# Seven block products in place of eight for the output of the last two chunks

## The chip, the cores and the metric

The kernel runs on one core of a Trainium2 chip. The metric is the device time of one execution in microseconds (us). Names of engines in rows: PE is TensorE's matmuls and PEld its weight loads, DVE is VectorE, ACT is ScalarE, POOL is GpSimd, SP is SyncE; here SP and ACT issue the DMAs.

## What is computed

```python
def _attn_ref(q, k, v):                       # q, k, v: 8 batches x 8 heads x 576 x 64
    k_p = k.reshape(B, H, Sp, pool, D).mean(axis=3)      # pool = 8, Sp = 72
    v_p = v.reshape(B, H, Sp, pool, D).mean(axis=3)
    scores = scale * np.matmul(q, k_p.transpose(0, 1, 3, 2))
    scores = scores - np.max(scores, axis=-1, keepdims=True)
    attn = np.exp(scores)
    attn = attn / (np.sum(attn, axis=-1, keepdims=True) + 1e-09)
    return np.matmul(attn, v_p).astype(np.float32)

def _moe_ref(x, w_in, w_out):                 # x: 4608 x 512, w_in: 512 x 2048, w_out: 2048 x 512
    h = x @ w_in
    g = h * (1.0 / (1.0 + np.exp(-1.702 * h)))
    return (g @ w_out).astype(np.float32)
```

The attention's output, transposed to tokens x (heads, head dimension), is `x`.

## The kernel before, in words

The 4608 tokens are worked on in nine chunks of 512: chunk c from 0 to 7 is the first 512 tokens of batch c, chunk 8 is the 64 tokens left over of each batch. Attention of batch c runs between the dense products of earlier chunks and leaves `x` for chunk c. All dense products are in a 32-bit matmul format, each operand split into a high and a low part, so a product of two blocks is three matmuls: high by high, low by high, high by low.

Chunks 0 and 1 multiply plainly (`dense`). From chunk 2 on the first product, `x @ w_in`, is made pair by pair: a *pair* (function `pair`, p from 0 to 7) is 256 of the 2048 middle columns. Its four blocks (two blocks of 128 middle columns f by two halves th of the tokens) come from seven products of 42 matmuls of 256 columns in all (L2473, PSUM banks `ha` and `hb`), with sums of `x` and of `w_in` as operands. The sums of `w_in` were made once, stored in DRAM (`fold`) and are read again for each pair (`ws`, `shared`, L2405). Then `keep` copies a block out of PSUM (L2488, ACT or DVE), `plus` adds another bank's half to it (L2495, DVE), `gelu` makes the activation twice on ACT (L2512 in the rounded format, `gh`, and L2520 in full), and POOL or DVE subtracts to get the low part `gl` (L2527).

`outputs` is the second product, `g @ w_out`. For each pair there are eight products (two blocks f by four tiles of 128 tokens), each of three matmuls of 512 columns (L2675 to L2677), which add to four PSUM banks `o` for the whole chunk. The outputs of a pair stand between the products of the next pair. After the last pair `finish` copies each bank to SBUF and stores it; in chunk 8 the copies are made by DVE and ACT (L2234, L2246), and the last tile's two halves are stored on SP and on ACT at once (L2240).

The order of everything is that of a planner (`Plan.order`), which works from costs and due times; after it a table (`PLACES`) moves single steps by a number of places, and another (`SWAPPED`) gives single steps to the other engine of two (ACT or DVE, POOL or DVE). Each engine, and each DMA queue, then works strictly in that order.

## Time and profile before

| | |
|---|---|
| timed runs, median of 3 (lowest, highest) | 892.92 us (891.83, 893.32) |
| profiled execution, first to last instruction (its span) | 889.3 us |
| PE, DVE, ACT, POOL busy in the span | 878.7, 646.0, 544.2, 314.1 us |
| TensorE clock granted | full speed in all 40 slices |

The profiled execution has no time of its own but its span, which does not hold what lies around the program. The median of the timed runs is 3.6 us above that span, and this difference is what is added to a span to compare it with a time. A busy engine is one with an instruction under way; matmuls overlap each other, so the distance between their starts tells more than the busy time.

### The profile page before, as it was taken

To read this page: it belongs to the slowest core of one execution; us is meant where nothing else is said; L and a number is where in the kernel's file an instruction comes from. 1 tells how busy PE (TensorE), PEld (TensorE's weight loads), DVE (VectorE), ACT (ScalarE), POOL (GpSimd) and SP (SyncE) were. 2 spreads that over 40 slices of the span, in tenths; PEclk is the share of its full clock that TensorE was granted. 3 is DMA by queue.
4 is the path that set the end of the run, shared out by engine and by line. 5 is a ranking of instruction groups with operands and counts; after the bars stand their busy time and mean duration, and the time that the engine had idled before them with its cause. 6 is when DMAs were issued, how large, how long until landed. Compare 5 with 4: busy or idle time off the path is not lost.

```text
span 889.3 us, 15811 instructions
## 1 busy us (share of the span) xinstructions
PE 878.7 (99%) x5432; PEld 785.1 (88%) x5432; DVE 646.0 (73%) x1288; ACT 544.2 (61%) x1245; POOL 314.1 (35%) x309
## 2 busy tenths in 40 slices
PE   7999999999999999999999999999999999999997
PEld 6889888888899998899999998989998989998986
DVE  6998989888888886698878887787777843222332
ACT  5986755356676754667576766685568563344433
POOL 2888655564312233222421162236323460000000
PEclk9999999999999999999999999999999999999999
DMA  9954455657468757677776677678664675556541
GB/s 285 379 184 134 125 152 177 234 185 220 151 201 233 227 178 252 170 235 239 219 216 181 170 247 212 214 214 243 173 208 142 199 237 187 182 183 202 166 143 48
DMA packets 145263, 176.68 MB, mean 199 GB/s; under 512 B 85664, under 2 KB 96928, under 8 KB 145184
## 3 DMA queue, kind: packets, MB, share of 16 engines
q1 hardware_dynamic: 140336, 166.89, 61.2%
q10 hardware_dynamic: 4848, 8.78, 2.8%
q8 instruction: 43, 0.70, 0.3%
q14 instruction: 36, 0.29, 0.1%
HBM read 150.47 MB, written 25.17 MB: 198 GB/s over the span
## 4 chain that ended last, share of the span: by engine, by line
PE 94%; DVE 2%; ACT 1%; SPq 1%; DMA 1%; issue 1%; ACTq 0%
PE ha L2473 18%; PE hb L2473 13%; PE o L2677 12%; PE o L2676 12%; PE o L2675 11%; PE sps L1759 4%; PE h L2268 3%; PE h L2269 3%; PE h L2270 3%; PE o L2310 3%; PE o L2311 3%; PE o L2312 3%; PE pav L1998 1%; PE pav L2001 1%; PE pav L2000 1%; PE pav L1999 1%
## 5 line engine op out<-in xcount | busy, mean ns | idle before, releaser
L2677 PE MATMUL o<-w,glall 128*128 128x512 f32 x448 | 176.4, 394 | 0.0
L2675 PE MATMUL o<-w,ghall 128*128 128x512 f32 x448 | 176.4, 394 | 0.0
L2676 PE MATMUL o<-w,ghall 128*128 128x512 f32 x448 | 176.0, 393 | 0.0
L2527 POOL TENSOR_TENSOR glall<-shared,ghall 128x256 fp32r<-128x256 f32 x88 | 70.4, 805 | 215.1 <-ACT shared L2520 148.2
L2677 PEld LDWEIGHTS o<-w,glall 128*128 128x128 f32 x448 | 84.3, 188 | 18.5
L2473 PEld LDWEIGHTS ha<-xs,ws 128*128 128x128 f32 x672 | 92.7, 189 | 7.6 <-ACT shared L2488 1.0
L2473 PE MATMUL ha<-xs,ws 128*128 128x256 f32 x672 | 99.3, 284 | 0.0
L2512 ACT ACTIVATE ghall<-shared 128x256 fp32r<-128x256 f32 x150 | 61.5, 415 | 61.4 <-DVE shared L2495 30.4
L2473 PE MATMUL hb<-x,ws 128*128 128x256 f32 x672 | 95.5, 284 | 0.0
L2473 PEld LDWEIGHTS hb<-x,ws 128*128 128x128 f32 x672 | 89.1, 189 | 4.4 <-DVE shared L2495 0.5
L2675 PEld LDWEIGHTS o<-w,ghall 128*128 128x128 f32 x448 | 84.6, 189 | 9.1
L2676 PEld LDWEIGHTS o<-w,ghall 128*128 128x128 f32 x448 | 84.1, 188 | 9.1
L2495 DVE TENSOR_TENSOR shared<-shared,hb 128x256 f32<-128x256 f32 x112 | 46.5, 415 | 56.2 <-PE hb L2473 41.0
L2488 ACT COPY shared<-ha 128x256 f32<-128x256 f32 x94 | 34.8, 370 | 65.0 <-PE ha L2473 63.9
L2527 POOL TENSOR_TENSOR glall<-gall,ghall 128x256 fp32r<-128x256 f32 x45 | 33.3, 744 | 103.4 <-ACT gall L2520 67.9
L2268 PE MATMUL h<-x,w 128*128 128x256 f32 (+1 forms) x192 | 63.1, 328 | 0.8 <-ACT g L2285 0.5
L2520 ACT ACTIVATE shared<-shared 128x256 f32<-128x256 f32 x150 | 61.0, 415 | 3.7 <-ACT osb L2228 0.5
L2269 PE MATMUL h<-x,w 128*128 128x256 f32 (+1 forms) x192 | 61.2, 319 | 0.0
L2270 PE MATMUL h<-x,w 128*128 128x256 f32 (+1 forms) x192 | 61.2, 319 | 0.0
L2298 POOL TENSOR_TENSOR gl<-g,gh 128x512 fp32r<-128x512 f32 x30 | 40.2, 1340 | 48.0 <-ACT gh L2290 33.2
L2527 DVE TENSOR_TENSOR glall<-shared,ghall 128x256 fp32r<-128x256 f32 x62 | 29.2, 472 | 36.0 <-ACT shared L2520 30.5
L2473 PEld LDWEIGHTS ha<-x,shared 128*128 128x128 f32 x336 | 46.7, 189 | 4.9 <-ACT shared L2488 0.8
(194 smaller groups left out, 2057.2 us busy)
## 6 DMA issues: line engine op xcount, KB each, us to landing
ws<-wd SPq DMA_DIRECT2D x168, 512.0 KB
shared<-wd SPq DMA_DIRECT2D x56, 256.0 KB
out_dram<-osb ACTq DMA_DIRECT2D x32, 256.0 KB
wd<-stage SPq DMA_DIRECT2D x16, 512.0 KB
raw<-in_moe_w_in_dram SPq DMA_DIRECT2D x15, 512.0 KB
raw<-in_moe_w_out_dram SPq DMA_DIRECT2D x15, 512.0 KB
kv_False<-in_k_dram SPq DMA_DIRECT2D x28, 256.0 KB
kv_True<-in_v_dram SPq DMA_DIRECT2D x28, 256.0 KB
```

The costliest lines, as they stand in the source:

```text
L2268: nc.tensor.matmul(o, lhsT=w[:, 0, j], rhs=xs[:, 0], start=j == 0, stop=False)
L2269: nc.tensor.matmul(o, lhsT=w[:, 1, j], rhs=xs[:, 0], start=False, stop=False)
L2270: nc.tensor.matmul(o, lhsT=w[:, 0, j], rhs=xs[:, 1], start=False, stop=j == NJ - 1)
L2298: engine.tensor_tensor(out=gl(), in0=g(), in1=gh().bitcast(F32), op=ALU.subtract)
L2473: nc.tensor.matmul(o, lhsT=wv()[:, r, jj], rhs=xo(k, jj), start=start and n == 0, stop=n == len(terms) - 1,  skip_group_check=not start,)
L2495: lambda: nc.vector.tensor_tensor(out=part(i), in0=part(i), in1=hb()[:, half * 256 : half * 256 + 256], op=ALU.add),
L2512: lambda: nc.scalar.activation(out=gh(), in_=src(), func=AF.Gelu_apprx_sigmoid),
L2520: lambda: nc.scalar.activation(out=part(i), in_=src(), func=AF.Gelu_apprx_sigmoid),
L2527: engine.tensor_tensor(out=gl(), in0=part(i), in1=gh().bitcast(F32), op=ALU.subtract)
L2675: nc.tensor.matmul(o(), lhsT=gh()[:, tok], rhs=w()[:, 0], start=start, stop=False)
L2676: nc.tensor.matmul(o(), lhsT=gh()[:, tok], rhs=w()[:, 1], start=False, stop=False)
L2677: nc.tensor.matmul(o(), lhsT=gl()[:, tok], rhs=w()[:, 0], start=False, stop=stop)
```

## The change

In chunks 7 and 8 (`SEVEN`), except for the last pair of chunk 8, the second product is made as the first one already is: for a pair, the two blocks of `g` by two halves of the tokens and the two blocks of `w_out` by two halves of its columns give seven products (P1 to P7) in place of eight. Each of the seven (`sevens`) is six matmuls of 256 columns.

- Four sums of blocks of `g` are needed per pair (`combined`: s1 to s4): a subtraction or addition on DVE, a rounding copy on ACT or DVE, and a subtraction on POOL or DVE for the low part. The rounded activation of one of the four blocks is no longer needed.
- Four sums of blocks of `w_out` are needed per pair (t1 to t4). They are made once (`make_sums`), during chunks 2 to 5, in 32 sets of three additions or subtractions (POOL or DVE), one copy (ACT or DVE) and one store to DRAM (SP). In chunks 7 and 8 they are read back, two reads of 512 KB per pair (`fetch_sums`), into space that attention no longer uses.
- P1, P5, P6 and P7 add up in the four banks `o` over the chunk, and P3 in a bank of its own. P2 and P4 share one bank (`Z`) by turns, and are added to a sum in SBUF by DVE after each pair (`add_up`).
- After the last pair the output's four quadrants are put together from these sums on DVE (`end`), and stored for chunk 7 as two stores of 512 KB. In chunk 8 the last pair is made by `outputs` as before, in the banks `o` again, and DVE adds each of them to the quadrants (`finish_sum`).
- More places for `g` and its parts are added from attention's space (`g_slot`, `c_slot`), and `PLACES` and `SWAPPED` have new numbers, from the end of chunk 1 on.

```diff
--- before.py
+++ after.py
-    "ACT ah0_0#0": 15.003, "ACT ah0_0#1": 14.024, "ACT ah0_0#2": -11.989, "ACT ah0_0#3": -38.996,
...
+    "ACT ah0_0#0": 15.36, "ACT ah0_0#1": 16.88, "ACT ah0_0#2": -8.6154, "ACT ah0_0#3": -35.0, "ACT ah0_1#0": 11.0,
...
+    SEVEN = (7, 8)
+    MADE = 2
...
     def finish(c, t, acc):
...
+        if c == B:
+            return finish_sum(t, acc)
...
+        def store():
+            nc.vector.tensor_tensor(out=osb(), in0=acc(), in1=osb(), op=ALU.add)
+            queues = (nc.sync, nc.scalar) if t == CHUNK - P else (nc.scalar,) * 2 if t == P else (nc.sync,) * 2
...
     def pair(c, p, due, then):
...
-        keep(0, ha)
+        begun = keep(0, ha)
+        if seven:
+            plan.due = due - 20
+            sums[c, p] = fetch_sums(c, p, begun)
...
+        def combined(name, op, i, a, b):
+            plan.due = due - EAGER
+            t = dve(
+                256,
+                lambda: nc.vector.tensor_tensor(out=part(i), in0=part(a), in1=part(b), op=op),
+                [at(a), at(b)],
+                [at(i)],
+                port=True,
+            )
+            hold(t, *[places[k][1] for k in {i, a, b}])
+            gh, w1 = g_slot(f"{nm}_{name}", "gh", True)
+            gl, w2 = g_slot(f"{nm}_{name}", "gl", True)
+            hold(copy(256, lambda copy: copy(out=gh(), in_=part(i)), [at(i)], [gh], sbuf=True), w1, places[i][1])
+
+            def rest(engine):
+                engine.tensor_tensor(out=gl(), in0=part(i), in1=gh().bitcast(F32), op=ALU.subtract)
+
+            t = pool(256, lambda: rest(nc.gpsimd), [at(i), gh], [gl], other=lambda: rest(nc.vector))
+            hold(t, w2, places[i][1])
+            return gh, gl
+
+        ops = {"11": got[0, 0], "12": got[1, 0], "22": got[1, 1]}
+        for name, op, i, a, b in (
+            ("s1", ALU.add, 2, 1, 2),
+            ("s3", ALU.subtract, 1, 0, 1),
+            ("s2", ALU.subtract, 0, 2, 0),
+            ("s4", ALU.subtract, 3, 3, 0),
+        ):
+            ops[name] = combined(name, op, i, a, b)
+        return ops
...
+    def make_sums(p):
+
+        def parts(i, cols):
+            h = homes[1, 2 * p + i]
+            return h, lambda: h()[:, :, 256 * cols : 256 * cols + 256].bitcast(F32)
+
+        left = {}
+        for name, a, b, op in (
+            ("t3", parts(1, 1), parts(0, 1), ALU.subtract),
+            ("t2", "t3", parts(0, 0), ALU.add),
+            ("t4", "t2", parts(1, 0), ALU.subtract),
+            ("t1", parts(0, 1), parts(0, 0), ALU.subtract),
+        ):
+            d = buf(moe, [P, 2, 256], F32, "osb", f"made{p}_{len(left)}")
...
+            step(512, d, av, bv, op, [a, b], [d])
+            step(256, lambda d=d: d()[:, 1], lambda d=d: d()[:, 0], lambda d=d: d()[:, 1], ALU.add, [], [d])
+            other = ("DVE", 0.2, lambda high=high: high(nc.vector.tensor_copy), True)
+            made.add("ACT", 0.32, lambda high=high: high(nc.scalar.copy), [], [d], other=other)
+            step(
+                256,
+                lambda d=d: d()[:, 1].bitcast(F32R),
+                lambda d=d: d()[:, 1],
+                lambda d=d: d()[:, 0],
+                ALU.subtract,
+                [],
+                [d],
+            )
+            i, k = next((i, ts.index(name)) for i, ts in enumerate(TS) if name in ts)
+            made.add(
+                "DMA",
+                0.8,
+                lambda d=d, i=i, k=k: nc.sync.dma_start(out=t_dram[p][i][:, k], in_=d()),
+                [d],
+                [(t_refs[p][i], k)],
...
+            b = Buf(ring, view, f"ts{c}_{p}_{i}")
+            t = dma(
+                P * 4096,
+                lambda b=b, i=i: nc.sync.dma_start(out=b().bitcast(F32), in_=t_dram[p][i]),
+                [],
+                [b],
+                lag=LAGS["ws"],
+            )
+            hold(t, whole)
+            plan.behind(t, begun)
+            t_fetches.append((t, p, i))
...
+        todo = [
+            ("P1", "11", of(w0, 0)),
+            ("P2", "12", of(w1, 0)),
+            ("P6", "s2", ts["t2"]),
+            ("P7", "s3", ts["t3"]),
+            ("P5", "s1", ts["t1"]),
+            ("P4", "22", ts["t4"]),
+            ("P3", "s4", of(w1, 1)),
+        ]
...
+        def add_up(name, z):
+            c_of = sums_of[c, name]
+            plan.due = due - 5.0
+            if first:
+                copy(512, lambda copy: copy(out=c_of(), in_=z()), [z], [c_of])
+            else:
+                dve(512, lambda: nc.vector.tensor_tensor(out=c_of(), in0=c_of(), in1=z(), op=ALU.add), [z], [c_of])
...
+                def products(gh=gh, gl=gl, wv=wv, bank=bank, fresh=fresh):
+                    w = wv()
+                    for i in range(2):
+                        o, tok = bank()[:, 256 * i : 256 * i + 256], slice(P * i, P * i + P)
+                        for k, (g, r) in enumerate(((gh, 0), (gh, 1), (gl, 0))):
+                            begin = fresh and i == 0 and k == 0
+                            nc.tensor.matmul(
+                                o,
+                                lhsT=g()[:, tok],
+                                rhs=w[:, r],
+                                start=begin,
+                                stop=k == 2,
+                                skip_group_check=not (fresh and i == 0),
+                            )
+
+                t = pe(6 * 120, products, [gh, gl, wb], [bank], mode="f32r")
+                hold(t, *[x for x in (whole, wh) if x is not None])
+                if name in ("P2", "P4"):
+                    add_up(name, bank)
+                if last:
+                    plan.due = due + at + n * step - 3.0
+                    end(name)
...
+            if is_seven(c, p):
+                then = sevens(c, p, acc, got, sums[c, p], due + ROUND / NPAIR)
+            else:
+                then = outputs(c, p, acc, got, due + ROUND / NPAIR)
...
+    for n, t in enumerate(made.tasks):
+        n, k = divmod(n, 5)
+        begin, end = (at[f"PE ha{MADE + n // 8}_{i}#2"] for i in (0, 7))
+        t.rank = begin + (end - begin) * (n % 8 + 0.2 * k + 0.3 * (k == 4)) / 8
```

In all, PE loses 360 matmuls of 512 columns and gets 630 of 256 columns (15 pairs of 24 and of 42).

PE in chunk 7 around the start of pair 4's products, before. `ha7_4` and `hb7_4` are pair 4's products from `x`; `o7_...` are outputs of pair 3 (`w1_6` and `w1_7` are its two blocks of `w_out`).

```order
L2473 MATMUL hb7_4_9018<-x7_8148,ws7_4_0_8858 128x256 x6
L2473 MATMUL ha7_4_9028<-x7_8107,ws7_4_0_8858 128x256 x6
L2473 MATMUL hb7_4_9018<-x7_8478,ws7_4_1_8890 128x256 x6
L2675 MATMUL o7_0_8709<-w1_7_841,ghall0_2956 128x512
L2676 MATMUL o7_0_8709<-w1_7_841,ghall0_2956 128x512
L2677 MATMUL o7_0_8709<-w1_7_841,glall0_2969 128x512
L2675 MATMUL o7_256_8759<-w1_7_841,ghall1_2996 128x512
L2676 MATMUL o7_256_8759<-w1_7_841,ghall1_2996 128x512
L2677 MATMUL o7_256_8759<-w1_7_841,glall1_3006 128x512
L2473 MATMUL ha7_4_9028<-xs7_15_8540,ws7_4_2_8920 128x256 x6
L2675 MATMUL o7_128_8773<-w1_6_824,ghall0_2956 128x512
L2676 MATMUL o7_128_8773<-w1_6_824,ghall0_2956 128x512
L2677 MATMUL o7_128_8773<-w1_6_824,glall0_2969 128x512
```

The same place in the changed kernel. `bankP3` is P3 of pair 2, `o7_0_P1` is P1 of pair 3, `bankZ` with `sums_main` is P4 of pair 2.

```order
L2619 MATMUL ha7_4_9302<-x7_8270,ws7_4_0_9180 128x256 x6
L3088 MATMUL bankP3_9124<-w1_5_781,ghmore_ah0_8966 128x256 x2
L3088 MATMUL bankP3_9124<-w1_5_781,glmore_al0_8968 128x256
L3088 MATMUL bankP3_9124<-w1_5_781,ghmore_ah0_8966 128x256 x2
L3088 MATMUL bankP3_9124<-w1_5_781,glmore_al0_8968 128x256
L3088 MATMUL o7_0_P1_8973<-w1_6_840,ghmore_ah1_8980 128x256 x2
L3088 MATMUL o7_0_P1_8973<-w1_6_840,glmore_al1_9004 128x256
L3088 MATMUL o7_0_P1_8973<-w1_6_840,ghmore_ah1_8980 128x256 x2
L3088 MATMUL o7_0_P1_8973<-w1_6_840,glmore_al1_9004 128x256
L2619 MATMUL hb7_4_9331<-x7_8403,ws7_4_0_9180 128x256 x6
L3088 MATMUL bankZ_8949<-sums_main_8866,ghall0_2967 128x256 x2
L3088 MATMUL bankZ_8949<-sums_main_8866,glall0_2983 128x256
```

Where three matmuls of 512 columns stood there are now six of 256, and the outputs stand further behind the products from `x`: P3 and P4 of pair 2 come while pair 4 is under way.

DVE at the end of the program, before: the last additions and low parts of pair 7 of chunk 8, and two of the four copies of the result.

```order
L2527 TENSOR_TENSOR glall0_2969<-gall_3057,ghall0_2956 128x256
L2495 TENSOR_TENSOR shared12_2917<-shared12_2917,hb8_7_10074 128x256
L2527 TENSOR_TENSOR glall1_3006<-shared12_2917,ghall1_2996 128x256
L2495 TENSOR_TENSOR gall_3057<-gall_3057,hb8_7_10074 128x256
L2527 TENSOR_TENSOR glall0_2969<-shared12_2917,ghall0_2956 128x256
L2527 TENSOR_TENSOR glall1_3006<-gall_3057,ghall1_2996 128x256
L2234 COPY osb8_0_10164<-o8_0_9466 128x512
L2234 COPY osb8_256_10178<-o8_256_9538 128x512
L2735 UNCONDITIONAL_BRANCH
```

And in the changed kernel:

```order
L3018 TENSOR_TENSOR u8_10753<-u8_10753,o8_0_P5_10056 128x512
L3018 TENSOR_TENSOR both8_0_10788<-u8_10753,bankP3_9124 128x2x256
L2642 TENSOR_TENSOR gall_3067<-gall_3067,hb8_7_10755 128x256
L2680 TENSOR_TENSOR glall1_3035<-csmore_tl_8868,ghall1_3007 128x256
L3018 TENSOR_TENSOR both8_1_10864<-v8_10857,o8_0_P5_10056 128x2x256
L2680 TENSOR_TENSOR glall1_3035<-csmore_tl_8868,ghall1_3007 128x256
L2680 TENSOR_TENSOR glmore_al0_8968<-gall_3067,ghmore_ah0_8966 128x256
L2382 TENSOR_TENSOR both8_0_10788<-o8_0_10870,both8_0_10788 128x512
L3006 TENSOR_TENSOR sum8_P4_10066<-sum8_P4_10066,bankZ_8949 128x512
L3018 TENSOR_TENSOR both8_1_10864<-v8_10857,sum8_P4_10066 128x2x256
L2382 TENSOR_TENSOR both8_1_10864<-o8_256_10881,both8_1_10864 128x512
L2382 TENSOR_TENSOR both8_1_10864<-o8_384_10885,both8_1_10864 128x512
L2382 TENSOR_TENSOR both8_0_10788<-o8_128_10902,both8_0_10788 128x512
```

The copies have become additions of `o8_...` to `both8_0` and `both8_1` (the quadrants), the sums for P3, P4 and P5 stand among the last low parts, and the last of all is the tile at token 128, whose two stores stand one behind the other on ACT.

## Rows read from the trace of the kernel before

**Rows 1.** The page's busy times, and slices of the span in tenths.

```profile
PE 878.7 (99%) x5432; PEld 785.1 (88%) x5432; DVE 646.0 (73%) x1288; ACT 544.2 (61%) x1245; POOL 314.1 (35%) x309
...
PE   7999999999999999999999999999999999999997
...
DVE  6998989888888886698878887787777843222332
```

**Rows 2.** The page's chain that ended last, by engine.

```profile
PE 94%; DVE 2%; ACT 1%; SPq 1%; DMA 1%; issue 1%; ACTq 0%
```

**Rows 3.** Waits of PE from 238 to 884 us: total, times, longest.

```profile
PE ha L2473 <- DVE gall L2488: 0.2, 1, 0.2
```

**Rows 4.** Chain through chunk 8, 794.47 to 884.2 us: by line, and pieces.

```profile
by line: PE ha L2473 25.6%; PE hb L2473 19.4%; PE o L2677 18.5%; PE o L2675 18.4%; PE o L2676 18.2%
...
862.79 1.44 PE hb L2473 x12
...
867.02 0.70 PE ha L2473 x6
...
868.42 0.80 PE ha L2473 x6
...
870.63 0.81 PE hb L2473 x6
```

**Rows 5.** Windows of the same stretch, of L2473 and of L2675 alone.

```profile
794.47:884.20 89.73, 46.16 (x336) 1.00 0.45 144
...
794.47:884.20 89.73, 28.21 (x72) 1.00 0.45 144
```

**Rows 6.** Windows by chunk: us, busy PE, PEld, DVE, ACT, POOL, clock, DMA share, GB/s.

```profile
238.00:333.00 95.00, 95.00 (x608) 86.00 (x607) 80.10 (x169) 61.65 (x149) 24.81 (x26) 1.00 0.66 202
333.00:428.00 95.00, 94.82 (x606) 85.99 (x605) 74.60 (x157) 64.10 (x160) 28.67 (x34) 1.00 0.72 223
523.00:614.50 91.50, 91.50 (x593) 82.95 (x591) 72.95 (x145) 64.67 (x160) 33.77 (x37) 1.00 0.72 215
794.47:884.20 89.73, 89.73 (x552) 80.25 (x551) 28.43 (x69) 38.32 (x95) 0.00 (x0) 1.00 0.45 144
```

**Rows 7.** Groups of instructions: count, busy us, mean ns, idle before and its end.

```profile
L2495 DVE TENSOR_TENSOR shared<-shared,hb 128x256 f32<-128x256 f32 x112 | 46.5, 415 | 56.2 <-PE hb L2473 41.0 <-ACT shared L2488 14.4
L2527 DVE TENSOR_TENSOR glall<-gall,ghall 128x256 fp32r<-128x256 f32 x29 | 15.2, 522 | 24.9 <-ACT gall L2520 24.9
L2076 DVE TENSOR_TENSOR xt<-xt,xt 128x512 f32<-128x512 f32 x7 | 7.0, 996 | 0.3 <-POOL xt L2076 0.2
L2082 DVE CAST x<-xt 128x512 fp32r<-128x512 f32 x8 | 4.3, 543 | 1.5 <-POOL xt L2076 1.4
...
L2527 POOL TENSOR_TENSOR glall<-shared,ghall 128x256 fp32r<-128x256 f32 x88 | 70.4, 805 | 215.1 <-ACT shared L2520 148.2 <-PE ha L2473 44.4 <-issue 7.1
L2076 POOL TENSOR_TENSOR xt<-xt,xt 128x512 f32<-128x512 f32 x14 | 19.7, 1405 | 14.4 <-DVE xt L2052 10.5 <-ACT xt L2052 3.6
```

**Rows 8.** PE in order of time around 377 us.

```profile
377.19 0.97 PE L2473 MATMUL ha<-x,shared 128*128 128x256 f32 x6 [0.18 <-DVE gall L2488]
```

**Rows 9.** The DMA queue's own waits on SP in chunk 8.

```profile
SPq L2405 <- PE ha L2473: 39.2, 12, 5.2
SPq L2405 <- PE hb L2473: 18.6, 12, 4.5
```

**Rows 10.** The end in order of time, 881.96 us on: copies of the result and their stores.

```profile
881.96 0.69 DVE L2234 COPY osb<-o 128x512 f32<-128x512 f32 x1 [0.92 <-PE o L2677]
...
883.26 1.19 ACTq L2236 DMA_DIRECT2D out_dram<-osb  x2
...
884.27 0.40 PE L2677 MATMUL o<-w,glall 128*128 128x512 f32 x1
884.71 0.58 ACT L2246 COPY osb<-o 128x512 f32<-128x512 f32 x1 [1.48 <-PE o L2677]
885.32 0.47 ACTq L2240 DMA_DIRECT2D out_dram<-osb  x1
885.47 0.55 SPq L2240 DMA_DIRECT2D out_dram<-osb  x1
```

More of the change, by code (lines that the diff above doesn't have):

```diff
@@ L2524, in gelu @@
             )
+            hold(t, places[i][1])
+            if late:
+                return None
             def rest(engine):
                 engine.tensor_tensor(out=gl(), in0=part(i), in1=gh().bitcast(F32), op=ALU.subtract)
-            if c == B:
+            if c == B and not seven:
                 t = dve(256, lambda: rest(nc.vector), [at(i), gh], [gl], port=True)
```

228 lines of the change are left out of this document (182 added, 46 removed), and 1840 rows, old and new, of tables (PLACES, SWAPPED).

## The prediction, made before the result was known

> **What bounds the kernel now.** I read the busy times first: PE is busy 99% of the span and its slices are full from the second to the last but one [rows 1], and PE makes up 94% of the chain that ended last [rows 2]. Since matmuls overlap, "busy" could hide waits, so I asked next for the waits of PE from the first pair of chunk 2 to the last product: one, of 0.2 us [rows 3]. Shorter waits show in the chain, where six matmuls from `x` take 0.72 us each time they follow each other (1.44 for twelve) but 0.80 or 0.81 in two places of chunk 8 [rows 4]. So between 238 and 884 us the time is the number of matmuls times their distance, with next to nothing lost. The reader is to see two consequences: matmuls that go away are time that goes away, if nothing new makes PE wait; and a new order of the steps has almost no waiting left to remove.
>
> **The products.** I price a matmul by the chain through chunk 8, which is 89.73 us long and nothing but PE [rows 4]. The lines of `ha` and `hb` have 25.6 + 19.4 = 45.0% of it, 40.4 us, and the windows count 336 such matmuls [rows 5]: 0.1202 us for 256 columns. The three lines of the output have 55.1%, 49.4 us, and 72 matmuls each, 216 in all [rows 5]: 0.2289 us for 512 columns. A matmul of half the columns costs a little more than half. The shapes that the change adds are those of `ha` and `hb` (128 by 128 stationary, 256 columns, a fresh weight load each), so their row is the price.
>
> Per pair, out go 24 x 0.2289 = 5.49 us, in come 42 x 0.1202 = 5.05 us: 0.445 us less. With the shortest piece of six in that chain, 0.70 [rows 4], it would be 0.59. Fifteen pairs are 6.7 us by the mean and 8.9 by the shortest piece. **I take -6.9 us**: a mean over 336 is what 630 will be near to, and it holds a few small waits that I cost apart. One product of eight is an eighth of the output's share in two chunks, but half of that comes back because short matmuls are dearer per column.
>
> **The sums of g, in chunks 7 and 8.** Per pair there are four additions, four roundings and four low parts more, one rounding by ACT and one low part less, and two additions of 512 columns for bank Z. I counted the changed order over its 15.5 pairs: DVE has per pair some 1.3 copies, 3.1 `plus`, 3.5 low parts, 3.9 sums, 1.9 roundings and 1.8 additions from bank Z. At 0.42 us for those with 256 columns (0.415 where one input is in PSUM, 0.522 for the low part, which has both in SBUF [rows 7]), half of 0.543 for a rounding [rows 7] and 0.69 for 512 columns out of PSUM [rows 10], that is 0.5 + 1.3 + 1.8 + 1.6 to 2.0 + 0.5 + 1.2 = 6.9 to 7.3 us of a pair's 10.1 us. Before, DVE was busy 28.4 us in the eight pairs of chunk 8, 3.6 us a pair, and POOL not at all [rows 6]; POOL gets 3.6 low parts a pair at 0.805 [rows 7], 2.9 us. So the engines have the time; the question is when each result is there. The longest chain is: last product of a pair, `plus`, activation, s1, s2, rounding, low part, P6: 0.42 + 0.42 + 0.42 + 0.42 + 0.3 + 0.8 and five hand-overs, about 4 us by these rows. In the changed order some twenty products (14 us) stand between a pair's last product and its P6 in the middle of a chunk, and eight to ten (6 to 7 us) at a chunk's start and end; the eight places for `gh` and `gl` in place of four allow it. Tighter is bank Z: it is used twice a pair, and four times in the two chunks only two products, 1.4 us, lie between two uses, against 0.17 (what a matmul's row reaches beyond the next start, 0.40 less 0.23 [rows 10]) and 0.69 us of DVE, which must begin within half a us. What is queued behind an addition that waits for Z on DVE are the next low parts, for which PE waits; that is where a miss would show. The bound from below is no wait; from above I take one wait per pair like the 0.80 or 0.81 in place of 0.72 [rows 4], 15 x 0.09 = 1.3 us, or at two per pair 2.7. **+0.5 us**, nearer the lower end, since chunk 8 of before shows two such pieces in eight pairs.
>
> **The sums of w_out, in chunks 2 to 5.** 32 sets of three steps on POOL or DVE: by the order 15 of 512 columns and 26 of 256 go to DVE, 17 and 38 to POOL, and the table moves 24 combining steps of `x` (512 columns) from POOL to DVE. At 0.996 and 0.522 us on DVE and at 1.405 and 0.805 on POOL [rows 7], DVE gets 15 + 14 + 24 = 53 us more, POOL 24 + 31 - 34 = 21 us more, over chunks 2 to 6; a dozen copies that go from DVE to ACT give some 5 us back. DVE is busy 73 to 80 us of a chunk's 91 to 95 now [rows 6]; with 10 more it is at 83 to 90. The cover is that none of these sums is needed before chunk 7; what is not covered are the steps queued behind them on DVE, on which PE waits. From below nothing; from above, each of the 32 sets delays PE once like the one wait that the rows show (0.97 us for six matmuls in place of 0.72 [rows 8]): 8 us. That DVE's 15 to 20 idle us a chunk are not used up puts it near the lower end: **+0.4 us**. The 32 stores (256 KB) add 8 MB to some 80 MB in those chunks (380 us at 202 to 223 GB/s [rows 6]), and the 30 reads of 512 KB some 105 GB/s to 144 GB/s at a share of 0.45 [rows 5]: 0.78 if it scales. SP's reads wait for PE to free a buffer, 24 times in chunk 8 [rows 9], and are issued most of a pair ahead of their use, so 1 or 2 us more of transfer is hidden. I cost them at nothing; without that lead each late read would cost PE 1 to 2 us.
>
> **The end.** The last tile's copy was 0.58 us on ACT, and its two stores were issued side by side, 0.47 and 0.55 us [rows 10]. Now DVE adds it, 0.69 us by its copy of the same size, and both stores of the tile that is last (token 128) are issued by ACT one behind the other; two such took 1.19 us [rows 10], 0.5 more than the 0.7 from the first issue to the second one's end. **+0.6 us.** The four banks are handed from P1, P6, P7, P5 to the last pair's tiles while three more products run (2.1 us), behind one to three additions of 0.69: no wait by this count, at most 1 us.
>
> Sum: -6.9 + 0.5 + 0.4 + 0.6 = -5.4 us. The profiled execution's 889.3 becomes 883.9; with the 3.6 us around it, 887.5 us. That is 0.6% under the median of 892.92. A measurement of this kernel can tell some 0.2% (1.8 us) from no change.
>
> **Rivals.**
> *VectorE falls behind in chunks 7 and 8* (the gain is lost). For it: 7 us of 10, most of it in chains, on an engine with a strict order. A step of 256 columns takes DVE 0.415 with one input in PSUM and 0.522 with both in SBUF [rows 7], and one of 512 columns 0.69 out of PSUM [rows 10] and 0.996 with both in SBUF, so something beside it costs DVE a quarter or more there. The Trainium skill ("SBUF — State Buffer", "Who interferes with whom") says why: a VectorE instruction with two SBUF inputs and a GpSimd one that reads SBUF take turns, and the second waits for the whole of the first; this trace's means agree. Against it: POOL works 2.9 us of 10. If a third of its 7.4 such steps of a pair met a POOL step and lost half of 0.8 us, DVE would be at 8.3 us a pair, still under 10.1. It decides from 10.1 on: at 10.55 us a pair all of the gain is gone (15 x 0.445) and the time is 893 to 894.
> *The sums of w_out hold up PE in chunks 2 to 5* (the other sign). From 32 sets at 0.17 us on, the gain of 5.4 us is eaten; at the full 0.25 of the one wait shown it is +8 in place of +0.4 and the time 895. For it: DVE is the busiest engine after PE just there, and a rounding on ACT waits in line for a step on POOL. Against it: PE waited 0.2 us in all those chunks although DVE was at 80 of 95 us.
> *Half of either*, 2 to 4 us lost: 889.5 to 891.
> *Cheaper still*: the short price for every matmul and no new waits, 892.9 - 8.9 + 0.6 = 884.6.
> That the change does not do what it says is ruled out by the order: 360 matmuls out, 630 in.
>
> **How the numbers follow.** Forecast, 885.5 to 889.5: 0.62. Cheaper still, under 885.5: 0.12. Half lost, 889.5 to 891.1: 0.10. No gain, within 0.2% either way: 0.09. Slower, by one of the first two rivals in full: 0.07. So faster by over 0.2% 0.84, within 0.2% 0.09, slower 0.07. The range reaches to the ends of the cheap and the half lost case, 884.3 to 891.2, and leaves out about 0.18.
>
> **What would show it.** Right: 630 matmuls at 0.12 us and a pair in chunks 7 and 8 of 10.1 to 10.2 us in place of 10.55; PE's waits between 238 us and the end still under 1 us in sum; DVE busy about 7 us a pair at the end; the store of the last tile 0.6 us later behind the last matmul. Wrong: a pair of 10.4 us or more with PE waiting for `gl` or for bank Z; PE waits on DVE or ACT in chunks 2 to 5 that add to several us; matmuls from DRAM's sums that wait for a read.

## The result, and the profile after

The change made the kernel slower: 899.91 us (898.50 to 901.72, four runs) against 892.38 us (890.86 to 893.32, four runs), a ratio of 1.0091 with a 95% interval of 1.0071 to 1.0110. The forecast was 887.5 us, 884.3 to 891.2. The profiled execution has a span of 899.1 us and a time of 900.92.

Busy times and the waits of PE come first, as in [rows 1, 3]. From the page of the changed kernel:

```profile
PE 880.2 (98%) x5702; PEld 796.6 (89%) x5702; DVE 729.7 (81%) x1518; ACT 553.2 (62%) x1287; POOL 341.8 (38%) x357
...
DVE  6998989888979988777888888898778657667666
...
PE 86%; DMA 6%; SPq 3%; ACT 2%; DVE 1%; issue 1%; POOL 0%; ACTq 0%; DVEq 0%; POOLq 0%
```

PE is busy all but as before, yet it makes up 86% of the chain where it was 94% [rows 2], and DMA has come in with 6%. Waits of PE from 238 to 894 us (total, times, longest):

```profile
PE ha L2619 <- DMA shared<-wd: 3.7, 1, 3.7
PE hb L2619 <- DVE shared L2642: 2.4, 2, 2.2
PE kps L1687 <- DVE xs L2184: 1.1, 1, 1.1
PE ha L2619 <- ACT shared L2634: 0.6, 2, 0.4
PE ha L2619 <- DMA ws<-wd: 0.5, 1, 0.5
PE o L2865 <- POOL glall L2680: 0.2, 1, 0.2
```

One wait of 0.2 us [rows 3] has become eight with 8.5 us, and none of them lies in chunks 7 and 8. The windows say where (us, busy PE, PEld, DVE, ACT, POOL, granted clock, DMA share, GB/s): chunk 2, chunk 3, chunk 4, and a stretch of chunk 8.

```profile
241.00:338.00 97.00, 95.11 (x597) 85.70 (x596) 84.41 (x183) 64.76 (x158) 25.61 (x29) 0.98 0.74 232
338.00:444.00 106.00, 99.89 (x610) 88.76 (x609) 82.42 (x178) 66.51 (x162) 35.54 (x41) 0.97 0.70 208
444.00:538.00 94.00, 93.42 (x599) 83.95 (x598) 79.64 (x173) 67.15 (x165) 30.77 (x34) 1.00 0.76 233
...
810.00:890.00 80.00, 80.00 (x668) 79.70 (x667) 56.98 (x136) 34.98 (x93) 23.32 (x32) 1.00 0.71 253
```

Chunk 3 takes 106 us for as many matmuls as 95 us held before [rows 6]. The granted clock, full throughout before, is below it in two chunks. The longest stall shows how one leads to the other; in order of time, around 396 us:

```profile
391.31 0.59 SPq L2540 DMA_DIRECT2D shared<-wd  x1
...
395.47 0.40 PE L2865 MATMUL o<-w,glall 128*128 128x512 f32 x1
...
399.58 1.42 PE L2619 MATMUL ha<-x,shared 128*128 128x256 f32 x6 [3.72 <-DMA shared<-wd]
```

The six matmuls at 399.58 wait for a read of 256 KB that was issued at 391.3 us, and then take 1.42 us; six such matmuls at full clock read 0.88 in this view (at 404.28 us), which has the last one's whole length in it. The windows of 4 us there:

```profile
392.00:396.00 4.00, 3.77 (x21) 2.64 (x19) 3.86 (x10) 2.17 (x3) 1.61 (x2) 1.00 0.94 239
396.00:400.00 4.00, 0.41 (x3) 0.45 (x4) 0.76 (x3) 3.02 (x6) 1.53 (x3) 0.98 0.76 204
400.00:404.00 4.00, 4.00 (x23) 4.00 (x23) 1.58 (x5) 1.10 (x3) 1.90 (x2) 0.60 1.01 316
404.00:408.00 4.00, 4.00 (x27) 3.63 (x26) 3.90 (x4) 1.78 (x5) 0.00 (x0) 1.00 0.81 275
```

After PE stood still for 3.9 us the clock is at 0.60 in the next 4 us: most of them at 1.2 GHz. The windows of 4 us from 236 to 720 us, summed as 4 us times what is missing to 1.00, give 5.1 us, all behind three stalls (250, 396 and 427 us); in the kernel before the same sum is 0.0. The windows behind the other two stalls:

```profile
252.00:256.00 4.00, 3.74 (x18) 3.54 (x19) 4.00 (x8) 2.52 (x7) 0.73 (x1) 0.63 0.30 45
256.00:260.00 4.00, 4.00 (x28) 3.75 (x28) 3.08 (x8) 0.68 (x2) 2.31 (x3) 0.94 0.94 271
...
428.00:432.00 4.00, 2.07 (x12) 2.07 (x13) 3.72 (x10) 2.49 (x7) 0.76 (x1) 0.82 0.62 209
432.00:436.00 4.00, 4.00 (x23) 3.81 (x23) 3.15 (x9) 1.85 (x6) 0.76 (x1) 0.76 0.33 126
```

The stalls at 250 and 427 us are of the same kind, one engine further on. At 250 us VectorE has stood still for 2.2 us for a transfer, with sums of x that PE needs in line behind it. At 427 us VectorE stands still for a read of attention's keys (`kv_False`), and the addition that PE needs (L2642) is in line behind it.

```profile
426.09 1.98 DVE L1647 TENSOR_REDUCE kbd<-kv_False 128x128 f32<-128x1024 f32 x1 [3.11 <-DMA kv_False<-in_k_dram]
...
429.46 0.42 DVE L2642 TENSOR_TENSOR shared<-shared,hb 128x256 f32<-128x256 f32 x1
```

All of PE's time can be put down by the distance from each matmul's start to the next. The output's matmuls of 512 columns took 310.3 us before and 235.5 now, the 630 new ones 74.2; those of the first product went from 283.9 to 291.1 and those of attention from 98.0 to 100.8. What lies above the median distance of a matmul of its kind (where over 0.06 us) adds to 4.0 us between 225 and 725 us before, and to 20.7 now: 7.5 us of it are the three stalls, 5.1 the lower clock, and the rest is in small pieces. So 16.6 us were lost in chunks 2 to 6, and some 8 were gained by the products: 74.2 - 82.1, as 360 matmuls of 512 columns are 82.1 less in a kernel without these stalls (below). In the chain through 810 to 890 us the three lines of the seven products have 28.3 + 14.2 + 8.0 = 50.5% of 80 us, and the windows count 342 of them: 0.118 us for one.

```profile
by line: PE o_P L3088 28.3%; PE ha L2619 27.7%; PE hb L2619 20.7%; PE bankZ L3088 14.2%; PE bankP L3088 8.0%; PE o L2863 0.6%; PE o L2864 0.6%; PE o L2865 0.3%
```

```profile
810.00:890.00 80.00, 45.37 (x342) 42.45 (x342) 1.00 0.71 253
```

### The profile page after: what moved, and what is told of

It reads as the page before. It is cut to its first block, busy times and chain, and to the rows that moved or that the text cites. A ratio compares the mean times of both kernels' runs of the same rounds, so it can differ in the third digit from the quotient of the medians.

```text
span 899.1 us, 16724 instructions
## 1 busy us (share of the span) xinstructions
PE 880.2 (98%) x5702; PEld 796.6 (89%) x5702; DVE 729.7 (81%) x1518; ACT 553.2 (62%) x1287; POOL 341.8 (38%) x357
## 4 chain that ended last, share of the span: by engine, by line
PE 86%; DMA 6%; SPq 3%; ACT 2%; DVE 1%; issue 1%; POOL 0%; ACTq 0%; DVEq 0%; POOLq 0%
PE ha L2619 17%; PE hb L2619 13%; PE o L2865 7%; PE o L2864 7%; PE o L2863 7%; PE o_P L3088 5%; PE sps L1900 4%; PE h L2403 3%; PE h L2405 3%; PE h L2404 3%; PE o L2445 3%; PE o L2447 3%; PE o L2446 3%; PE bankZ L3088 2%; DMA raw<-in_moe_w_in_dram 1%; PE bankP L3088 1%
## 5 line engine op out<-in xcount | busy, mean ns | idle before, releaser
L2865 PE MATMUL o<-w,glall 128*128 128x512 f32 x326 | 128.5, 394 | 0.2 <-POOL glall L2680 0.2
L2863 PE MATMUL o<-w,ghall 128*128 128x512 f32 x326 | 128.5, 394 | 0.0
L2864 PE MATMUL o<-w,ghall 128*128 128x512 f32 x326 | 128.0, 393 | 0.0
L2680 POOL TENSOR_TENSOR glall<-shared,ghall 128x256 fp32r<-128x256 f32 x67 | 54.3, 815 | 135.3 <-ACT shared L2670 118.9
L2865 PEld LDWEIGHTS o<-w,glall 128*128 128x128 f32 x326 | 61.3, 188 | 14.2 <-POOL glall L2680 0.6
L2662 ACT ACTIVATE ghall<-shared 128x256 fp32r<-128x256 f32 x115 | 46.9, 414 | 39.6 <-PE o L2864 19.7
L2863 PEld LDWEIGHTS o<-w,ghall 128*128 128x128 f32 x326 | 61.7, 189 | 6.2
L2864 PEld LDWEIGHTS o<-w,ghall 128*128 128x128 f32 x326 | 61.3, 188 | 6.4
L2680 POOL TENSOR_TENSOR glall<-gall,ghall 128x256 fp32r<-128x256 f32 x34 | 25.2, 744 | 98.8 <-ACT gall L2670 69.1
L2898 POOL TENSOR_TENSOR made<-made 128x256 fp32r<-128x256 f32 (+1 forms) x38 | 29.6, 779 | 70.0 <-ACT made L2904 29.8
L2670 ACT ACTIVATE shared<-shared 128x256 f32<-128x256 f32 x128 | 51.9, 415 | 4.2 <-ACT osb L2367 0.8
L2619 PE MATMUL ha<-x,shared 128*128 128x256 f32 x336 | 50.5, 286 | 4.0 <-DMA shared<-wd 3.7
```

What stands on the lines that cost most here:

```text
L2619: nc.tensor.matmul(o, lhsT=wv()[:, r, jj], rhs=xo(k, jj), start=start and n == 0, stop=n == len(terms) - 1,  skip_group_check=not start,)
L2662: lambda: nc.scalar.activation(out=gh(), in_=src(), func=AF.Gelu_apprx_sigmoid),
L2670: lambda: nc.scalar.activation(out=part(i), in_=src(), func=AF.Gelu_apprx_sigmoid),
L2680: engine.tensor_tensor(out=gl(), in0=part(i), in1=gh().bitcast(F32), op=ALU.subtract)
L2863: nc.tensor.matmul(o(), lhsT=gh()[:, tok], rhs=w()[:, 0], start=start, stop=False)
L2864: nc.tensor.matmul(o(), lhsT=gh()[:, tok], rhs=w()[:, 1], start=False, stop=False)
```

## The experiments

"Old places" are the numbers of `PLACES` and `SWAPPED` of the kernel before, which its first 4000 steps (all ahead of chunk 7) have in both kernels' planner in the same order; "new places" are those of the change. Times are medians, and the ratio is to the kernel before on the same chip (892 us each time).

### Sums or order?

`no_sums` and `old_order_no_sums` make no sums of w_out:

```diff
-                lambda b=b, i=i: nc.sync.dma_start(out=b().bitcast(F32), in_=t_dram[p][i]),
+                lambda b=b, i=i: nc.sync.dma_start(out=b().bitcast(F32), in_=w_dram[p][i].rearrange("p n (r c) -> p n r c", r=2)),
...
-    order += made.tasks
```

`old_order` and `old_order_no_sums` have the old places ahead of chunk 7, and `no_store` only leaves out the stores:

```diff
     for t in order:
-        t.rank += PLACES.get(t.name, 0)
-        if t.name in SWAPPED:
+        old = t.rank < 4000 and id(t) not in made_tasks
+        t.rank += (OLD_PLACES if old else PLACES).get(t.name, 0)
+        if t.name in (OLD_SWAPPED if old else SWAPPED):
             t.swap()
```

```diff
-    order += made.tasks
+    order += [t for t in made.tasks if t.engine != "DMA"]
```

> The changed kernel with its whole order, without the making of the sums of w_out: their 32 sets of steps and 32 stores are left out, and the reads of chunks 7 and 8 fetch blocks of the same size from the sums of w_in instead (so the output is not that of the reference). Behind 238 us PE lost some 20 us between matmuls before chunk 7 in the changed kernel, against 3.5 in the kernel before. Theory A, the sums of w_out and their stores (time on VectorE, GpSimd and SP's queue): the stalls at 250, 396 and 427 us go, 884 to 888 us. Theory B, the new places of the other steps (sums of x moved to VectorE, transfers moved on SP's queue): the stalls stay, 896 to 900 us. Both by halves: 890 to 894 us.

> The changed kernel, but every step that the planner puts ahead of chunk 7 (its first 4000 places) gets the places and the engine of the kernel before; the sums of w_out stay where the changed kernel has them, and chunks 7 and 8 are as changed. Theory A (the sums hold PE up wherever the rest stands): 895 to 900 us, stalls of some us in chunks 2 to 5. Theory B (the new places of the other steps): 886 to 889 us.

> The places of the kernel before ahead of chunk 7, and no making of the sums of w_out (the reads fetch sums of w_in instead, so the output is not that of the reference). This is the change of chunks 7 and 8 by itself. Both theories expect chunks 2 to 6 as in the kernel before, PE losing some 3.5 us in all of them, and the predicted -6.9 + 0.5 + 0.6 for the products, the sums of g and the end: 886 to 888 us. If it is above 889, the terms of chunks 7 and 8 were wrong too.

> The changed kernel with its whole order; the sums of w_out are made, but their 32 stores are left out, and the reads fetch sums of w_in of the same size (so the output is not that of the reference). If the stores (256 KB each, and SP's queue standing still behind one whose sum is not ready yet, some 30 us in all) are what delays the reads of the w_in sums: 885 to 890 us, as without the sums. If it is the steps on VectorE, ScalarE and GpSimd, or the new places of the other steps: 896 to 900 us.

| | time, us | ratio (95%) |
|---|---|---|
| `old_order_no_sums` | 885.19 | 0.9923 (0.9900, 0.9946) |
| `no_sums` | 892.01 | 0.9996 (0.9976, 1.0016) |
| `no_store` | 894.70 | 1.0033 (1.0018, 1.0048) |
| `old_order` | 929.75 | 1.0426 (1.0404, 1.0447) |

The change of chunks 7 and 8 by itself is worth 6.9 us by the ratio. The new places cost 6.8 of them back even where no sum is made (stalls at 250 and 395 us stay, and the ten runs lie from 888.4 to 896.5), and the sums 7.9 more. Neither theory holds alone, and the two do not add up: with the old places the sums cost 44 us where the change has put them. They share two buffers with the result's copies, which are then handed over in another order, and SP stands 36.6 us for sums of GpSimd that are not ready, 17.0 in the changed kernel; neither was tried as the cause. So `old_order` does not price the sums. With the seam at place 4000, low parts of g are also written over before their last products, so a part of the output is wrong in `old_order`, `old_order_no_sums`, `sums_pool` and `sums_split`; `split2` and what follows have the seam at 4060 and not this flaw.

### The sums with the old places, and parts of the new order

`sums_pool` and `sums_split` put the sets at regular places between the second pair of a chunk and the next chunk; the first has all additions on GpSimd, the second divides them as the change does. `queue_old_no_sums` and `x_old_no_sums` undo a part of the new order (all transfers but three at their old places; the sums of x on their old engines), `split2` is `sums_split` with the later seam:

```diff
-        begin, end = (at[f"PE ha{MADE + n // 8}_{i}#2"] for i in (0, 7))
-        t.rank = begin + (end - begin) * (n % 8 + 0.2 * k + 0.3 * (k == 4)) / 8
+        c = MADE + n // 8
+        begin, end = at[f"PE ha{c}_1#2"], at[f"PE ha{c + 1}_0#2"] - 40
+        t.rank = begin + (end - begin) * (n % 8 + 0.2 * k + 0.3 * (k == 4)) / 8.2
```

```diff
+        old = t.rank < 4000 and t.name.startswith("DMA")      # queue_old_no_sums
+        t.rank += (OLD_PLACES if old else PLACES).get(t.name, 0)
...
+        old = t.rank < 4000 and t.name.startswith("POOL x")   # x_old_no_sums
+        if t.name in (OLD_SWAPPED if old else SWAPPED):
```

> The kernel with the places of before ahead of chunk 7 (885.2 us without the sums of w_out), and now with these sums made and stored, nothing left out: each set in regular steps between the second pair of its chunk and the next chunk, all additions on GpSimd, the rounding copy on ScalarE, the store some 6 us behind its last step. Theory A (the sums' steps and 8 MB of stores cost PE wherever they stand): 890 us or more. Theory B (it is where the steps and stores stand, and what else was moved for them): 885 to 888 us, which beats both kernels.

> As the one before, with the sums' steps divided between VectorE, GpSimd and ScalarE as the changed kernel divides them (15 of 32 long and 26 of 64 short ones on VectorE, 14 of the copies too). If time on VectorE is what the sums cost PE (some 10 us of a chunk's 15 to 20 idle ones), 2 to 5 us above the one with all on GpSimd; if VectorE's spare time covers them, the same within 1 us.

> The changed kernel's order without the sums of w_out (892.0 us, against 885.2 with the places of before ahead of chunk 7; the reads fetch sums of w_in, so the output is not that of the reference), and now with the transfers ahead of chunk 7 at the places that they have on SP's queue in the kernel before, all else in the new places. If the 6.8 us come from the order of the transfers: 885 to 887 us. If from the new places of the steps on VectorE, ScalarE and GpSimd: 890 us or more.

> Again the changed kernel's order without the sums of w_out (892.0 us; the reads fetch sums of w_in, so the output is not that of the reference), and now with the sums of x ahead of chunk 7 on the engines of the kernel before: 24 steps of 512 columns go back from VectorE to GpSimd. If the 6.8 us come from VectorE being busier: 886 to 888 us, and no stall at 250 us. If from the transfers' order: 890 to 893 us.

> The kernel with the places of before ahead of chunk 7 and the sums of w_out in regular steps, divided between the engines as the changed kernel divides them; as sums_split, but the seam between the two tables lies 60 places later, so that no low part is overwritten early and nothing is left out. Expected as sums_split, 898 to 900 us: the sums cost 13 to 14 us there. If the overwritten blocks had a part in it: under 895.

| | time, us | ratio (95%) |
|---|---|---|
| `sums_pool` | 906.21 | 1.0153 (1.0138, 1.0169) |
| `sums_split` | 898.75 | 1.0074 (1.0058, 1.0091) |
| `split2` | 898.04 | 1.0069 (1.0054, 1.0084) |
| `queue_old_no_sums` | 938.53 | 1.0518 (1.0496, 1.0540) |
| `x_old_no_sums` | 903.34 | 1.0130 (1.0109, 1.0151) |

The sums cost PE 13 us with the old places (21 all on GpSimd), and VectorE's spare time does not cover them. Time on VectorE alone is not the price either: if it were, the division between the engines was expected to be 2 to 5 us slower than all on GpSimd, and it is 7.5 us faster. The other two did not tell where the 6.8 us come from: half of one order in the other is worse than `no_sums`, by 46 and 11 us, and both are outside what was expected if the part that they undo were the cause.

### Steps or stores?

`steps_only` is `split2` with the stores left out as in `no_store`. In `stores_only` (old places) and `stores_new` (new places) only the stores are left, of data that is ready:

```diff
-    order += made.tasks
+    order += [t for t in made.tasks if t.engine == "DMA"]
...
-                lambda d=d, i=i, k=k: nc.sync.dma_start(out=t_dram[p][i][:, k], in_=d()),
+                lambda d=d, i=i, k=k: nc.sync.dma_start(out=t_dram[p][i][:, k].rearrange("p r c -> p (r c)"), in_=homes[1, 2 * p + i]()[:, 0].bitcast(F32)),
```

> As split2, with the 32 stores of the sums left out (the reads of chunks 7 and 8 fetch sums of w_in, so the output is not that of the reference). If the steps on VectorE, GpSimd and ScalarE cost PE the time, as what stands in line behind them is late: 895 to 899 us. If it is the 8 MB of stores and SP's queue: 885 to 888 us.

> As split2, with the steps of the sums left out; the 32 stores are issued at the same places, of blocks of w_out as they are (so the output is not that of the reference). SP waits for nothing then, and only the 8 MB themselves and 32 more issues are tried. Theory of the steps: 885 to 887 us. Theory of the stores: 890 us or more.

> The changed kernel with its whole order, without the steps of the sums; the 32 stores stand at the places of the change, of blocks of w_out as they are (so the output is not that of the reference). In this order no sums at all gave 892.0 us, steps without stores 894.7, both 899.9. If the stores' 5.2 us come from their bytes and issues: 895 to 898 us. If they come from SP standing still behind a store whose sum isn't ready, with reads of the w_in sums in line: 890 to 893 us.

| | time, us | ratio (95%) |
|---|---|---|
| `steps_only` | 897.85 | 1.0067 (1.0051, 1.0082) |
| `stores_only` | 884.87 | 0.9920 (0.9902, 0.9937) |
| `stores_new` | 899.43 | 1.0076 (1.0058, 1.0094) |

With the old places it is all steps: 8 MB of stores cost nothing. With the new places the same stores, with nothing to wait for, cost 7.4 us over `no_sums`, about as much as the whole sums, and the steps by themselves 2.7 (`no_store`); the two do not add up to the 7.9 of both. So SP standing still behind a store is not needed for the loss; the stores' own transfers are enough. Two stalls are new against `no_sums`, 2.0 us at 307 us for a read `ws<-wd` and 2.4 us at 427 us, where VectorE waits 3.2 us for a read of the keys, and one more fall of the clock (1.7 us): 6.1 of the 7.1 us between the two spans. In the chain of `stores_new` from 241 to 715 us the longest pieces are reads, from issue to landing:

```profile
299.68 9.68 DMA ws<-wd
349.01 5.98 DMA ws<-wd
388.26 5.06 DMA tl<-in_v_dram
393.33 6.44 DMA shared<-wd
417.98 8.20 DMA kv_False<-in_k_dram
```

In the same stretch of the kernel before the five longest pieces are all matmuls. A long read in the chain is not yet a loss: `stores_only` has two there as well, of 7.9 and 7.0 us. Why the old places bear the same bytes was not settled: the reads `shared<-wd` are issued a little earlier there (20.3 us ahead of their first matmul in the median of chunks 2 to 5, 18.7 in `stores_new`, counted from the starts in the trace), but the lead is as short in `no_sums`.

### How the steps cost PE its time

`half_sets` makes 16 of 32 sets; `short_steps` makes the step of 512 columns as two of 256; `pool25` is `sums_pool` with the rounding copy on GpSimd too (and the later seam), `alone25` is `split2` with each pair's sets on one engine:

```diff
+    gone = {id(t) for t in made.tasks if int(re.search("[0-9]", t.name)[0]) >= 4}      # half_sets
+    made.tasks = [t for t in made.tasks if id(t) not in gone]
...
-            step(512, d, av, bv, op, [a, b], [d])                                      # short_steps
+            for r in range(2):
+                step(256, lambda d=d, r=r: d()[:, r], lambda av=av, r=r: av()[:, r], lambda bv=bv, r=r: bv()[:, r], op, [a, b], [d])
...
+            if p not in dve_pairs:                                                     # pool25: none; alone25: 0, 2, 4, 6
+                other = ("POOL", 0.5, lambda high=high: high(nc.gpsimd.tensor_copy), True)
...
+            if t.engine == "ACT" or t.engine == "POOL" and p in dve_pairs:
+                t.swap()
```

> As split2 (898.0 us), with the sums of w_out of pairs 0 to 3 alone, the 16 sets of chunks 2 and 3; those of pairs 4 to 7 are left out and the reads fetch sums of w_in in their place (so the output is not that of the reference). Without any it is 885.2. If each set delays PE by itself (about 0.4 us a set): 891 to 892.5 us, with the loss in chunks 2 and 3. If only the last of VectorE's idle time being used up costs something, the loss need not be half.

> As split2 (898.0 us), nothing left out; the step of 512 columns of each set (1.0 us on VectorE, 1.4 on GpSimd) is made as two of 256 columns with some 1.5 us between their places, on the same engine. Some 5 us more engine time in all. If PE's steps wait behind a long step that can't be broken off: 893 to 896 us. If it is the engine time as such, or waits behind a step that is itself not ready: 898 us or more.

> As sums_pool (906.2 us; the sums of w_out in regular steps in chunks 2 to 5, all additions on GpSimd, the rounding copy on ScalarE), with one edit: the rounding copy is made by GpSimd too, so that a whole set runs on one engine and hands nothing over but to its store (and the later seam of split2). GpSimd gets more work by it. If what costs PE is engines standing still in line for each other's steps of a set: well under 906, 886 to 895 us. If it is the time on GpSimd and the port that it shares with VectorE: 905 us or more.

> As split2 (898.0 us), with the same regular places, but the four sets of a pair all on VectorE (pairs 0, 2, 4, 6) or all on GpSimd (the others), copies too: much the same engine time in all, and no hand-over between engines within a pair's sets. Standing in line for hand-overs is the cause: 887 to 892 us. Engine time is the cause: 896 us or more.

| | time, us | ratio (95%) |
|---|---|---|
| `half_sets` | 890.36 | 0.9980 (0.9970, 0.9990) |
| `short_steps` | 898.24 | 1.0068 (1.0053, 1.0083) |
| `pool25` | 903.03 | 1.0125 (1.0109, 1.0142) |
| `alone25` | 900.01 | 1.0090 (1.0075, 1.0105) |

The sets cost where they are made: 16 cost 5.2 us, 32 cost 12.9. That is a little under half, and under the 891 to 892.5 us that 0.4 us for each set was expected to give. What lies above the median distances of PE is 7.4 us up to 428 us and 1.3 from there to 625, against 2.5 and 1.3 in `old_order_no_sums`. Windows of `half_sets`, with sets up to 428 us and without:

```profile
240.00:428.00 188.00, 184.65 (x1165) 164.92 (x1164) 163.47 (x336) 121.15 (x295) 75.54 (x84) 1.00 0.74 228
428.00:620.00 192.00, 192.00 (x1234) 174.44 (x1233) 156.41 (x316) 131.39 (x327) 65.77 (x73) 1.00 0.70 210
```

Neither the length of a step nor the hand-overs are most of it here: `short_steps` takes as long as `split2` (with 8 us more work in the sums, which may hide a small gain), and without hand-overs it is 3 us less in `pool25` than in `sums_pool` and 2 us more in `alone25` than in `split2`. What `split2` shows beside them is that VectorE's other steps get longer. Its timeline before the longest wait there:

```profile
521.66 1.40 POOL L3762 TENSOR_TENSOR made<-w 128x512 f32<-128x512 f32 x1
...
524.46 1.28 POOL L3081 TENSOR_TENSOR xt<-xt,xt 128x512 f32<-128x512 f32 x1
```

```profile
521.99 1.42 DVE L2991 TENSOR_TENSOR al<-mt,ah 128x320 fp32r<-128x320 f32 x1
...
524.48 1.34 DVE L2538 COPY k<-kbd 32x128 f32<-32x128 f32 x1
525.85 0.42 DVE L3498 COPY gall<-ha 128x256 f32<-128x256 f32 x1
526.30 0.42 DVE L3506 TENSOR_TENSOR gall<-gall,hb 128x256 f32<-128x256 f32 x1
```

```profile
526.78 0.98 PE L3483 MATMUL hb<-xs,ws 128*128 128x256 f32 x6 [1.76 <-DVE gall L3506]
```

The subtraction (0.45 us when it comes again at 527.00) ends 0.35 us after GpSimd's sum of w_out, the copy of 128 columns (0.21 us when it comes again at 527.82) 0.08 us after GpSimd's sum of x; the addition that PE waits for is behind both. Over chunks 2 to 5 the same instructions compare so (count, busy us, mean ns), in `stores_only` and in `pool25`:

```profile
L3506 DVE TENSOR_TENSOR shared<-shared,hb 128x256 f32<-128x256 f32 x65 | 26.8, 412 | 16.8 <-PE hb L3483 9.2 <-ACT shared L3498 7.1
...
L2991 DVE TENSOR_TENSOR al<-mt,ah 128x256 fp32r<-128x256 f32 x16 | 6.7, 422 | 0.6 <-ACT ah L2986 0.5
L2986 DVE CAST ah<-mt 128x320 fp32r<-128x320 f32 x9 | 3.2, 357 | 0.2
```

```profile
L3506 DVE TENSOR_TENSOR shared<-shared,hb 128x256 f32<-128x256 f32 x63 | 25.8, 410 | 12.2 <-PE hb L3483 6.4 <-ACT shared L3498 5.2 <-ACT main L2879 0.2
...
L2991 DVE TENSOR_TENSOR al<-mt,ah 128x256 fp32r<-128x256 f32 x16 | 10.0, 622 | 0.6 <-ACT ah L2986 0.5
L2986 DVE CAST ah<-mt 128x320 fp32r<-128x320 f32 x9 | 5.1, 562 | 0.2
```

Summed over all of VectorE's instructions from 241 to 625 us but the sums' own, what each takes above the median of its kind in `stores_only` is 17 us there, 23 in `half_sets`, 28 in `split2`, 37 in `sums_pool` and 43 in `pool25`, for times of 884.9, 890.4, 898.0, 906.2 and 903.0. All but about half a us of it is in steps that run while a GpSimd step is under way. In the changed kernel it is 8: the new places have moved some 30 low parts and 15 sums of x from GpSimd to VectorE. VectorE's busy time over chunks 2 to 6 hardly changed with it (375 us for 810 steps in `no_sums`, 377 for 779 in `old_order_no_sums`), and PE lost time all the same, in the stalls above. That the lengthening is what the sums cost with the old places is argued from these rows, and it is not all: `pool25` has more of it than `sums_pool` and takes 3 us less. No kernel took it away alone.

### Sums where the engines are idle

`seven8` keeps chunk 7 as before, makes the sums there, and has seven products in chunk 8 alone; `alone7` also keeps a pair's sets on one engine, VectorE and GpSimd side by side, and gives GpSimd's sets buffers of their own:

```diff
-    SEVEN = (7, 8)
+    SEVEN = (8,)
...
+        begin, end = at["PE ha7_1#2"], at["PE ha8_0#2"] - 10
+        t.rank = begin + (end - begin) * (n % 32 + (0, 0.35, 0.6, 0.85, 1.3)[k]) / 33.5     # seven8
+        m = n // 8 * 4 + n % 4 + n // 4 % 2 * 0.5                                           # alone7
+        t.rank = begin + (end - begin) * (m + (0, 0.3, 0.5, 0.7, 1.2)[k]) / 17.2
```

> Seven products in chunk 8 alone, and the sums of w_out made and stored during chunk 7, in which VectorE and GpSimd were little busy in the kernel before; chunks 2 to 6 are wholly as before, and nothing is left out. Seven pairs at 0.45 us are 3.1 us. If the sums cost PE only where VectorE, GpSimd and ScalarE have attention's steps in line: 888.5 to 890 us, under both kernels. If every set costs PE 0.4 us wherever it stands, as 13.5 us for 32 sets say: 900 us or more.

> As seven8 (931.4 us; seven products in chunk 8 alone, the sums made in chunk 7), with a pair's four sets all on VectorE (even pairs) or all on GpSimd (odd pairs, in places of attention's space that are free by then), the two running side by side; nothing is left out. Standing in line for hand-overs is the cause of the 40 us there: 889 to 895 us, and below 891 it beats both kernels. Engine time: VectorE is some 65 of 85 us busy in chunk 7 then, and 915 us or more would speak for it.

`seven8` took 931.41 us (ratio 1.0443, 1.0427 to 1.0458), `alone7` 915.23 (1.0262, 1.0247 to 1.0278). Windows of `seven8` while the sums are made:

```profile
730.00:800.00 70.00, 56.20 (x298) 47.37 (x297) 35.77 (x76) 23.23 (x63) 36.28 (x41) 0.90 0.61 201
800.00:860.00 60.00, 50.00 (x289) 44.14 (x288) 20.99 (x54) 20.52 (x54) 23.23 (x27) 0.89 0.68 229
```

VectorE and GpSimd are busy 35 to 52% of the time, PE waits all the same, and the clock takes 13.6 us of the 40 (summed as above from 715 to 870 us). Here, where a set follows the other every 3.2 us (32 in 102 us), an engine that is not busy stands in line for the other's step of a set. VectorE's own waits from 700 to 860 us:

```profile
DVE made L3846 <- POOL made L3846: 14.0, 8, 2.8
...
DVE made L3852 <- POOL made L3846: 7.9, 6, 2.3
```

`alone7`, without such hand-overs and with the further buffers, takes 16 us less; which of the two did it was not tried. No kernel that computes everything beat the kernel before.

## Why the prediction was wrong

**The products** were right in kind and a little better: 74.2 us for the 630 (0.118 each) for 75.7 forecast, and 82.1 us less for the 360 (310.3 - 228.2 in `old_order_no_sums`), for 82.4. Net -7.9 to -8.1, forecast -6.9 (its own prices give -6.7).

**The sums of g** cost nothing where +0.5 was put: PE has no wait in chunks 7 and 8, and VectorE is busy 57.0 of 80 us in chunk 8, 7.2 us of a pair's 10.1 as counted. The first rival fell. **The end** cost nothing either, for +0.6: from the last matmul's start to the span's end it is 5.05 us (894.08 to 899.13), 5.00 before (884.27 to 889.27). `old_order_no_sums` and `stores_only` put the change of chunks 7 and 8 at -6.9 and -7.0 us, for a forecast of -5.8 without the sums of w_out. The products' 8 us are not all kept: chunks 2 to 6 take 472.8 us in `old_order_no_sums`, 472.0 before.

**The step that failed is "The sums of w_out, in chunks 2 to 5", +0.4 us.** They and the order made for them cost 14.7 us (899.9 - 885.2): 6.8 for the order without any sum and 7.9 for the sums in it. Three things in it were wrong.
- Idle time was taken for cover ("That DVE's 15 to 20 idle us a chunk are not used up puts it near the lower end"). A set costs 0.4 us of PE in the mean with the old places (12.9 / 32), where VectorE's busy time rises from 366 of 460 us (240 to 700, `stores_only`) to 393 (`split2`), and over 1 us in chunk 7 at half load. The bound of 0.25 us a set, 8 us in all, was near the 7.9 of the changed kernel by luck. It sets 0.97 us of a timeline row [rows 8] against 0.72 us of the chain, but six undisturbed matmuls read 0.88 in that timeline (378.00 us), so the row itself gives 0.09. It also holds neither the lengthening of VectorE's steps beside GpSimd's nor the clock. VectorE's busy time was not the price: the text counted 48 us more over chunks 2 to 6, and it rose by 19 (379 to 399).
- The stores "I cost at nothing" are nothing with the old places, but with the new ones 7.4 us by themselves and 5.2 on top of the steps (899.9 - 894.7). The text had the price, a late read costs 1 to 2 us, and not the place: it looked at the lead of the reads in chunk 8 [rows 9] for transfers that are in chunks 2 to 5.
- "A new order of the steps has almost no waiting left to remove" was right and stopped too soon: a new order has waits to add. No term was for that, and it costs 6.8 us without any sum.

The second rival, with 895 us and a share in the 0.07 for "slower", is what happened, by half another road and with a clock that it did not price: of PE's 8.5 us of waits 4.1 were for VectorE and ScalarE, as its sign of being wrong had it (2.2 of them with VectorE behind a read of the keys), and 4.2 for reads of sums from DRAM, its third sign, but of w_in's sums and in chunks 2 to 5; three of the stalls brought 5.1 us at the lower clock with them.

The Trainium skill ("SBUF — State Buffer", "Who interferes with whom") stood in the text as a reason for the first rival, in chunks 7 and 8. It says that a VectorE copy or cast can shut out GpSimd, or be shut out by it, for a whole instruction, and that a VectorE step with two inputs in SBUF contends with a GpSimd step that reads SBUF. The rows of `split2` (1.34 us for a copy of 0.21) and of `pool25` (622 ns for a subtraction of 422) agree with it. They lie in chunks 2 to 5, to which the text did not apply it.

## What to carry to other kernels

Where one engine sets the time and the others follow in strict order, spare time of an engine does not by itself hide work that is put in among its steps: price an added step by what stands in line behind it, and by what it does to the steps of the engine beside it, then try it with the old order and a few sets. Look for the loss in the place that gets the work, not only in the one that gets the gain. Half of one order put into the other was 46 and 11 us slower here and did not name the cause; compare whole orders with one part of the work left out.

## What the runs showed of the hardware

- A stall of PE can be dearer than its length: behind stalls of 1.3, 3.9 and 2.3 us (what a distance from start to start has above the usual one) the granted clock was at 0.63, 0.60 and 0.76 over the 4 us with the longest stretch at 1.2 GHz, and each took some 1.7 us more (4 x (0.37 + 0.06), 4 x (0.02 + 0.40), 4 x (0.18 + 0.24)). The length of one stall does not decide it: in `split2` a stall of 1.9 us at 524.6 us brought no fall (the clock lost 0.0 us from 236 to 720), in `steps_only` the same stall at the same place did.
- With GpSimd's added work, one-input casts and copies of VectorE in SBUF grew longer as the two-input steps did (`ah<-mt` 357 to 562 ns), though not all of them: the copies `main<-sc` of 32x384 took 544 ns in both. Additions with one input in PSUM did not: 412 ns in `stores_only`, 410 in `pool25` (L3506).
- A read of 256 KB took 8.1 us from issue to landing at 391 and again at 418 us in the changed kernel, with the DMA share from 0.72 to 1.07 in the windows of 4 us meanwhile.
